# Attention units in runs of two: scores with queries, then values with projections, with single-buffered group data

## Chip, cores, metric

One core of one Trainium2 chip. The metric is the device time of one execution in microseconds (us), as the median of several executions. A difference counts as a change of speed only beyond 2%, but much of what follows is smaller than that and is read from the traces.

## The reference, cut

```
xn = layernorm(x)                                   # x: 2048 x 640
q  = xn @ wq                                        # 32 heads of 192
p  = softmax(q @ k.T * 192**-0.5)                   # the last 512 keys of the cache
s  = (p @ v) heads side by side @ wo                # 2048 x 6144 @ 6144 x 640
g  = silu((sigmoid(xn @ w_gate) * (xn @ w_up)) @ w_down)
out = x + s * g
```

## The kernel before

A preamble computes the gate `g`. The rest works in 32 *units*: 8 groups of 4 heads, times 4 blocks of 512 rows. For each unit the tensor engine (PE) does four kinds of work, each into one of four tiles `bank[0..3]` of PSUM, the memory that takes its results:

- `scores`: 8 groups of 6 matmuls on 64 rows of the array (two 64-row tiles work side by side: six matmuls in 0.65 us here, about 0.11 each; 34 full-row ones of the same width take 7.51 us in `a_warm` below, about 0.22 each); ScalarE (ACT) takes the exponential out of the bank.
- `queries` of a later unit: 6 halves of 10 matmuls, also on 64 rows; VectorE (DVE) copies the bank to `qT` (the cast).
- `values`: 4 heads of 16 matmuls on all 128 rows; DVE divides by the softmax sum.
- `project`: 4 tiles of 12 matmuls on 128 rows, which need the group's output weights `wo`; DVE adds to `acc`.

```python
for u in range(NU):
    ...
    if nxt:
        for i, what in enumerate(((0, 0), (1, 0), (0, 1), (1, 1), (2, 0), None, (2, 1), None)):
            scores(u, *sc[i], i % 2)                                    # banks 0, 1
            if what is not None:
                queries(u + 1, what[0], 2 + what[0] % 2, what[1])       # banks 2, 3, 2
    if b == 1 and g + 1 < NG:
        load_group(g + 1, nc.gpsimd)      # query weights, keys, values: two buffers
        load_wo(g + 1)                    # two buffers, POOL's queue
    if b == 2 and g + 1 < NG:
        turn_keys(g + 1)
    if nxt:
        order = (3, 2, 0, 1, 3, 2, 0, 1) if u else ...
        for q in range(4):
            values(u, q, order[2 * q])                                  # banks 3, 0, 3, 0
            if q == 3:
                turn_out(u)
            if u > 0:
                project(u - 1, q, order[2 * q + 1], nc.sync)            # banks 2, 1, 2, 1
# ... the last unit follows in an order of its own (the tail)
```

The softmax here doesn't subtract the row's maximum and nothing guards it: scores larger than these inputs give would overflow.

## Time and profile before

| before | |
|---|---|
| median of 3 runs | 931.14 us (930.13 to 931.9) |
| profiled span | 928.4 us |
| PE busy | 921.9 us (99%), clock 1.00 |
| DVE, ACT, POOL busy | 50%, 33%, 14% |
| one unit, start to start | 23.72 us |

The page's first part (busy time, share of the span, instructions) and its clock line:

```profile
PE 921.9 (99%) x8034; PEld 546.1 (59%) x8034; DVE 467.7 (50%) x739; ACT 304.9 (33%) x333; POOL 126.4 (14%) x154
...
PEclk9999999999999999999999999999999999999999
```

PE bounds the kernel. But 99% does not say that nothing is lost: the Trainium skill, "Perfetto Trace Analysis", opening note, calls matmul busy time a bad metric for the distance to the roofline, because matmuls are pipelined. The trace agrees: the windows view counts PE as busy in all 711.64 us from 187.83 to 899.47, drains included, and the drains described next cost time. So I read from start to start. The timeline of the kernel before, PE only, around both borders of a unit; columns are start, duration, what, and how many instructions:

```profile
280.99 1.79 PE L445 MATMUL bank<-wo_sb,oT 128*128 128x512 bf16 x12
282.71 0.82 PE L390 MATMUL bank<-qT,kT 64*128 64x512 bf16 x6
283.37 1.24 PE L408 MATMUL bank<-xnT,wq_sb 64*128 64x512 bf16 x10
284.45 0.81 PE L390 MATMUL bank<-qT,kT 64*128 64x512 bf16 x6
285.10 1.24 PE L408 MATMUL bank<-xnT,wq_sb 64*128 64x512 bf16 x10
...
291.35 1.46 PE L390 MATMUL bank<-qT,kT 64*128 64x512 bf16 x12
292.65 1.24 PE L408 MATMUL bank<-xnT,wq_sb 64*128 64x512 bf16 x10
293.73 0.81 PE L390 MATMUL bank<-qT,kT 64*128 64x512 bf16 x6
294.47 1.51 PE L425 MATMUL bank<-vbuf,E 128*128 128x193 bf16 x16
295.81 1.79 PE L445 MATMUL bank<-wo_sb,oT 128*128 128x512 bf16 x12
297.44 1.50 PE L425 MATMUL bank<-vbuf,E 128*128 128x193 bf16 x16
```

L390 is scores, L408 queries, L425 values, L445 projections. A projection tile takes 1.63 us inside its run (295.81 to 297.44) and 1.72 before scores (280.99 to 282.71). A score group takes 0.65 us inside its run (284.45 to 285.10; two take 1.30, 291.35 to 292.65) and 0.74 before values (293.73 to 294.47). So each turn between 64-row and 128-row work costs about 0.09 us. The Trainium skill, "TensorEngine Tiling (Array Packing)", Key Properties, says that changing the tiling mode drains the engine; this is what that looks like here. And one line of DVE in the same timeline, the cast of the unit's last query:

```profile
293.93 1.23 DVE L415 CAST qT<-bank 128x1024 bf16<-128x1024 f32 x1 [2.21 <-PE bank L408]
```

It holds its bank until 295.16, after the first value head has started (294.47). That does no harm, because here the cast empties bank 2 and the value head writes bank 3.

### The profile page before, as it was taken

Reading aid. Unit: us, or ns where it says so; the run is one execution under the profiler, and the core shown is the slowest. Engines: PE = TensorE matmul, PEld = TensorE weight load, DVE = VectorE, ACT = ScalarE, POOL = GpSimd, SP = SyncE. Lnnn points to the kernel's source line nnn. Section 1 sums busy time; section 2 is a strip of 40 time slices with the busy share of each in tenths; the row PEclk is TensorE's granted clock in tenths of the full one; section 3 lists DMA queues with packets and bytes.
Section 4 is the critical chain, followed back from the end, with each engine's and each line's share of the span. In section 5 each row is a group of like instructions: output and inputs, shape, how many; then the busy total and the mean of one; then the engine's idle time right before and its main releaser. Section 6 shows DMA issues by size and latency. Waiting matters only on the chain.

```text
span 928.4 us, 18112 instructions
## 1 busy us (share of the span) xinstructions
PE 921.9 (99%) x8034; PEld 546.1 (59%) x8034; DVE 467.7 (50%) x739; ACT 304.9 (33%) x333; POOL 126.4 (14%) x154
## 2 busy tenths in 40 slices
PE   9999999999999999999999999999999999999997
PEld 6445455565666556666556666556666666666665
DVE  5452522455545545445545445544555555445657
ACT  4222222433333333333333333333333333333341
POOL 1000100400010001000200020002000205555000
PEclk9999999999999999999999999999999999999999
DMA  9310420616224423443353433263326234422223
GB/s 319 79 29 1 130 43 1 196 36 146 52 53 78 129 60 60 78 96 92 61 77 62 119 69 78 57 124 69 78 49 131 69 68 77 93 63 64 53 64 102
DMA packets 157824, 76.69 MB, mean 83 GB/s; under 512 B 140801, under 2 KB 151665, under 8 KB 157745
## 3 DMA queue, kind: packets, MB, share of 16 engines
q1 hardware_dynamic: 149264, 45.90, 24.6%
q0 software_dynamic: 7248, 28.38, 10.7%
q8 instruction: 63, 1.03, 0.5%
q10 hardware_dynamic: 1232, 1.25, 0.4%
q14 instruction: 17, 0.13, 0.1%
HBM read 39.45 MB, written 2.62 MB: 45 GB/s over the span
## 4 chain that ended last, share of the span: by engine, by line
PE 98%; DVE 1%; DMA 1%; issue 0%; ACT 0%; DVEq 0%
PE bank L408 22%; PE bank L445 21%; PE bank L425 19%; PE bank L390 18%; PE bank L241 10%; PE bank L253 6%; PE bank L291 1%; PE bank L358 1%; DVE gate L454 1%; DMA wg_sb<-in_B_w_gate_dram 1%; DVE o_sb L449 1%; PE bank L221 0%; ACT xnT L227 0%; DVEq L530 0%; DVE warm L156 0%
## 5 line engine op out<-in xcount | busy, mean ns | idle before, releaser
L394 ACT ACTIVATE E<-bank 128x1024 bf16<-128x1024 f32 x256 | 257.8, 1023 | 477.4 <-PE bank L390 465.6
L408 PE MATMUL bank<-xnT,wq_sb 64*128 64x512 bf16 x1860 | 231.4, 376 | 0.0
L445 PE MATMUL bank<-wo_sb,oT 128*128 128x512 bf16 (+1 forms) x1536 | 228.6, 299 | 0.0
L390 PE MATMUL bank<-qT,kT 64*128 64x512 bf16 x1536 | 202.2, 377 | 0.0
L425 PE MATMUL bank<-vbuf,E 128*128 128x193 bf16 x2048 | 191.0, 247 | 0.0
L425 PEld LDWEIGHTS <-E 128*128 128x128 bf16 x2048 | 167.8, 98 | 24.2 <-issue 13.6
L415 DVE CAST qT<-bank 128x1024 bf16<-128x1024 f32 x93 | 113.9, 1225 | 132.8 <-PE bank L408 132.8
L445 PEld LDWEIGHTS <-oT 128*128 128x128 bf16 x1536 | 121.1, 98 | 76.8 <-issue 0.4
L408 PEld LDWEIGHTS <-wq_sb 64*128 64x128 bf16 x1860 | 97.3, 100 | 104.5
L390 PEld LDWEIGHTS <-kT 64*128 64x128 bf16 x1536 | 73.1, 94 | 90.0 <-issue 8.8
L431 DVE TENSOR_TENSOR o_st<-bank,rden 128x768 bf16<-128x768 f32 x128 | 122.6, 958 | 4.8 <-DVE rden L430 0.4
L460 DVE TENSOR_TENSOR acc<-bank,acc 128x640 f32<-128x640 f32 x96 | 79.2, 825 | 44.1 <-PE bank L445 44.1
L413 DVE COPY seen<-bank 128x2 f32<-128x2 f32 x93 | 14.8, 160 | 93.9 <-PE bank L408 93.8
L430 DVE RECIPROCAL rden<-bank 128x4 f32<-128x4 f32 x128 | 23.4, 182 | 71.0 <-PE bank L425 70.8
L241 PE MATMUL bank<-xnT,wg_sb 128*128 128x512 bf16 x220 | 54.7, 379 | 0.0
L241 PE MATMUL bank<-xnT,wu_sb 128*128 128x512 bf16 x220 | 54.7, 379 | 0.0
L253 PE MATMUL bank<-wd_sb,hT 128*128 128x512 bf16 (+1 forms) x384 | 52.8, 299 | 0.0
L247 DVE TENSOR_TENSOR hT<-bank,sig 128x512 bf16<-128x512 f32 x44 | 30.3, 689 | 42.2 <-ACT sig L244 42.2
L244 ACT ACTIVATE sig<-bank 128x512 bf16<-128x512 f32 x44 | 26.3, 597 | 68.4 <-PE bank L241 63.7
L106 POOL DMA_DIRECT2D vbuf<-in_A_v_cache_dram x28 | 20.9, 747 | 184.9 <-PE bank L425 184.9
L253 PEld LDWEIGHTS <-hT 128*128 128x128 bf16 x384 | 29.6, 98 | 23.2
L241 PEld LDWEIGHTS <-wu_sb 128*128 128x128 bf16 x220 | 21.5, 98 | 26.0
(51 smaller groups left out, 277.2 us busy)
## 6 DMA issues: line engine op xcount, KB each, us to landing
wo_sb<-in_A_wo_dram POOLq DMA_DIRECT2D x8, 960.0 KB, 7.3
wq_sb<-in_A_wq_dram POOLq DMA_DIRECT2D x7, 960.0 KB, 6.2
k_st<-in_A_k_cache_dram POOLq DMA_DIRECT2D x7, 768.0 KB, 7.9
vbuf<-in_A_v_cache_dram POOLq DMA_DIRECT2D x28, 192.0 KB, 3.0
row<-in_A_x_dram POOLq DMA_DIRECT2D x16, 160.0 KB, 2.6
oT<-o_st SPq DMA_TRANSPOSE x128, 2.6
x_sb<-in_A_x_dram SPq DMA_DIRECT2D x3, 640.0 KB, 11.0
wd_sb<-in_B_w_down_dram SPq DMA_DIRECT2D x1, 1920.0 KB, 14.5
```

The lines of the kernel that those rows point to most:

```text
L241: nc.tensor.matmul(bank[k][:, half, 0:r1 - r0], lhsT=w[:, c, f * P:(f + 1) * P], rhs=xnT[:, b, c, r0:r1], start=(c == 0), stop=(c == NCD - 1))
L244: nc.scalar.activation(sig[:, 0:r1 - r0], bank[k][:, 0, 0:r1 - r0], AF.Sigmoid)
L247: nc.vector.tensor_tensor(hT[b][:, f, r0:r1], bank[k][:, 1, 0:r1 - r0], sig[:, 0:r1 - r0], ALU.mult)
L253: nc.tensor.matmul(wide(k)[:, d0:d1], lhsT=hT[b][:, f, q * P:(q + 1) * P], rhs=wd_sb[:, f, d0:d1], start=(f == 0), stop=(f == NF - 1))
L390: nc.tensor.matmul(bank[k][:, i, :], lhsT=kT[r, pr, j, c * P:(c + 1) * P], rhs=q[r, pr * DJ + j, :], start=(j == 0), stop=(j == DJ - 1))
L394: nc.scalar.activation(E[u, pr][:, c, :, :], bank[k][:], AF.Exp, scale=scale_qk)
L408: nc.tensor.matmul(bank[k][:, half, :], lhsT=wq[r, c, col:col + DJ * (P - 1) + 1:DJ], rhs=xnT[r, b, c, :], start=(c == 0 and not second), ...
L415: nc.vector.tensor_copy(qT[u][:, 2 * m:2 * m + 2, :], bank[k][:])
L425: nc.tensor.matmul(o4[:, q, 0:DH + 1], lhsT=e[:, c, h % 2, q * P:(q + 1) * P], rhs=v[:, h, c, 0:DH + 1], start=(c == 0), stop=(c == KC - 1))
L431: nc.vector.tensor_tensor(o_st[u][:, :, h * DH:(h + 1) * DH], o4[:, :, 0:DH], rden[:].to_broadcast([P, TQ, DH]), ALU.mult)
L445: nc.tensor.matmul(wide(k)[:, d0:d1], lhsT=oT[u][:, cc, q * P:(q + 1) * P], rhs=wo[:, cc, d0:d1], start=(cc == 0), stop=(cc == GC - 1))
L460: nc.vector.tensor_tensor(acc[:, t, :], wide(k)[:, 0:D], acc[:, t, :], ALU.add)
```

## The change

Its intent: work in runs of two units, so that PE turns between the two kinds of work half as often. That needs more buffers for exponentials, queries and outputs, and the space comes from making all group data single-buffered. The query banks alternate between 2, 3, 2 and 3, 2, 3, so that the second unit of a run need not wait for the first one's last cast. The output weights move to SyncE's queue. The last two units form the tail.

```diff
-    vbuf = [pers.tile([P, 4, KC, VP], BF16, name=f"vbuf{i}") for i in range(2)]
+    vbuf = pers.tile([P, 4, KC, VP], BF16, name="vbuf")
 ...        (query weights, turned keys and staged keys likewise: one buffer)
-        nc.gpsimd.dma_start(d["wo"][:], wo_r[:, g * GC:(g + 1) * GC, :])
+        nc.sync.dma_start(d["wo"][:], wo_r[:, g * GC:(g + 1) * GC, :])
 ...        (the preamble computes the queries of units 0 and 1)
-    wo_pool = ctx.enter_context(tc.tile_pool(name="wo_pool", bufs=2))
+    wo_pool = ctx.enter_context(tc.tile_pool(name="wo_pool", bufs=1))
 ...        (E: 4 buffers, qT: 4, o_st: 2; rows of the residual: 2 instead of 4)
+    order = (3, 2, 0, 1)
+    for u0 in range(0, NU - 2, 2):
+        g, second = u0 // NB, u0 % NB != 0
+        more = g + 1 < NG
+        for u in (u0, u0 + 1):
             for i, what in enumerate(((0, 0), (1, 0), (0, 1), (1, 1), (2, 0), None, (2, 1), None)):
                 scores(u, *sc[i], i % 2)
                 if what is not None:
-                    queries(u + 1, what[0], 2 + what[0] % 2, what[1])
+                    queries(u + 2, what[0], 2 + (what[0] + u) % 2, what[1])
+        if more and not second:
+            load_wq(g + 1, nc.gpsimd)
+            load_keys(g + 1, nc.gpsimd)
+        if more and second:
+            turn_keys(g + 1)
+        for u in (u0, u0 + 1):
             for q in range(4):
+                if u0 > 0:
+                    values(u, q, order[2 * q % 4])
+                    project(u - 2, q, order[(2 * q + 1) % 4], nc.sync)
+                else:
+                    values(u, q, order[q])
+            turn_out(u)
+        if more and second:
+            load_values(g + 1, nc.gpsimd)
+        if g > 0 and not second:
+            load_wo(g)
+    u = NU - 2                                   # the tail: units 30 and 31
+    sc = [(v, *s) for v in (u, u + 1) for s in sc]
+    for i in range(6):
+        scores(*sc[i], order[i % 4])
+    for q in range(2):
+        project(u - 2, q, q, nc.sync)
 ...        (the rest of the scores, projections and values)
```

More of the change, by code (lines that the diff above doesn't have):

```diff
@@ L64 @@
     pers = ctx.enter_context(tc.tile_pool(name="pers", bufs=1, **rs))
-    load2 = ctx.enter_context(tc.tile_pool(name="load2", bufs=2, **rs))
     load1 = ctx.enter_context(tc.tile_pool(name="load1", bufs=1, **rs))
-    qpool = ctx.enter_context(tc.tile_pool(name="qpool", bufs=2, **rs))
+    qpool = ctx.enter_context(tc.tile_pool(name="qpool", bufs=4, **rs))
     bank = [psum.tile([P, 2, 512], F32, name=f"bank{i}") for i in range(4)]
@@ L91, with load_wq, load_keys, load_values @@
     grp = {}
-    def load_group(g, eng):
+    kv = slice(Sk - W, Sk)
+    def load_wq(g, eng):
         d = grp.setdefault(g, {})
-        d["wq"] = load2.tile([P, NCD, GW], BF16, name="wq_sb")
+        d["wq"] = load1.tile([P, NCD, GW], BF16, name="wq_sb")
         eng.dma_start(d["wq"][:], wq_r[:, :, g * GW:(g + 1) * GW])
-        kst = load1.tile([P, 4, KC, DH], BF16, name="k_st")
-        kv = slice(Sk - W, Sk)
-        eng.dma_start(
-            kst[:].rearrange("p h j d -> p h (j d)"),
-            A_k_cache[0, 4 * g:4 * g + 4, kv, :].rearrange("h (p j) d -> p h (j d)", j=KC),
-        )
-        d["v"] = vbuf[g % 2]
+    def load_keys(g, eng):
+        kp = load1.tile([P, 2, KC, DJ, P], BF16, name="k_perm")
+        for pr in range(2):
+            kst = load1.tile([P, 2, KC, DH], BF16, name="k_st")
+            h0 = 4 * g + 2 * pr
+            eng.dma_start(
+                kst[:].rearrange("p h j d -> p h (j d)"),
+                A_k_cache[0, h0:h0 + 2, kv, :].rearrange("h (p j) d -> p h (j d)", j=KC),
+            )
+            for i in range(2):
+                nc.gpsimd.tensor_copy(
+                    kp[:, pr, :, :, i * H2:(i + 1) * H2],
+                    kst[:, i, :, :].rearrange("p c (i j) -> p c j i", j=DJ),
+                )
+        grp[g]["kp"] = kp
+    def load_values(g, eng):
         for h in range(4):
             eng.dma_start(
-                d["v"][:, h, :, 0:DH],
+                vbuf[:, h, :, 0:DH],
                 A_v_cache[0, 4 * g + h, kv, :].rearrange("(p j) d -> p j d", j=KC),
             )
-        kp = load1.tile([P, 2, KC, DJ, P], BF16, name="k_perm")
-        for h in range(4):
-            nc.gpsimd.tensor_copy(
-                kp[:, h // 2, :, :, (h % 2) * H2:(h % 2) * H2 + H2],
-                kst[:, h, :, :].rearrange("p c (i j) -> p c j i", j=DJ),
-            )
-        d["kp"] = kp
     def load_wo(g):
@@ L120, in load_wo @@
         d["wo"] = wo_pool.tile([P, GC, D], BF16, name="wo_sb")
-        nc.gpsimd.dma_start(d["wo"][:], wo_r[:, g * GC:(g + 1) * GC, :])
+        nc.sync.dma_start(d["wo"][:], wo_r[:, g * GC:(g + 1) * GC, :])
     def turn_keys(g):
         d = grp[g]
-        d["kT"] = load2.tile([P, 2, DJ, W], BF16, name="kT")
+        d["kT"] = load1.tile([P, 2, DJ, W], BF16, name="kT")
         for pr in range(2):
@@ L175 @@
         make_identity(nc, ident[:])
-        for i in range(2):
-            nc.gpsimd.memset(vbuf[i][:, :, :, DH:DH + 2], 1.0)
+        nc.gpsimd.memset(vbuf[:, :, :, DH:DH + 2], 1.0)
         def dummy(n):
@@ L343 @@
             if b == 2:
-                load_group(0, nc.sync)
+                load_wq(0, nc.sync)
+                load_keys(0, nc.sync)
+                load_values(0, nc.sync)
             if b == 3:
@@ L359, in query_psum @@
                                  rhs=xnT[:, b, c, :], start=(c == 0), stop=(c == NCD - 1))
-        qT[0] = qpool.tile([P, 2 * DJ, TB], BF16, name="qT")
-        for m in range(DJ):
-            for half in range(2):
-                query_psum(0, 2 * m + half, k, half)
-            nc.vector.tensor_copy(qT[0][:, 2 * m:2 * m + 2, :], bank[k][:])
-            k = (k + 1) % 4
-    wo_pool = ctx.enter_context(tc.tile_pool(name="wo_pool", bufs=2))
+        for u in range(2):
+            qT[u] = qpool.tile([P, 2 * DJ, TB], BF16, name="qT")
+            for m in range(DJ):
+                for half in range(2):
+                    query_psum(u, 2 * m + half, k, half)
+                nc.vector.tensor_copy(qT[u][:, 2 * m:2 * m + 2, :], bank[k][:])
+                k = (k + 1) % 4
+    wo_pool = ctx.enter_context(tc.tile_pool(name="wo_pool", bufs=1))
     acc_pool = ctx.enter_context(tc.tile_pool(name="acc_pool", bufs=1))
-    e_pool = ctx.enter_context(tc.tile_pool(name="e_pool", bufs=2))
-    o_pool = ctx.enter_context(tc.tile_pool(name="o_pool", bufs=1))
+    e_pool = ctx.enter_context(tc.tile_pool(name="e_pool", bufs=4))
+    o_pool = ctx.enter_context(tc.tile_pool(name="o_pool", bufs=2))
     oT_pool = ctx.enter_context(tc.tile_pool(name="oT_pool", bufs=2))
     small = ctx.enter_context(tc.tile_pool(name="small", bufs=4))
-    fin = ctx.enter_context(tc.tile_pool(name="fin", bufs=4))
+    fin = ctx.enter_context(tc.tile_pool(name="fin", bufs=2))
     acc = acc_pool.tile([P, NT, D], F32, name="acc")
@@ L419, in values @@
     def values(u, h, k):
-        g = u // NB
-        v, e = grp[g]["v"], E[u, h // 2]
+        e = E[u, h // 2]
         o4 = wide(k).rearrange("p (q n) -> p q n", q=TQ)
@@ L425, in values @@
                 nc.tensor.matmul(o4[:, q, 0:DH + 1], lhsT=e[:, c, h % 2, q * P:(q + 1) * P],
-                                 rhs=v[:, h, c, 0:DH + 1], start=(c == 0), stop=(c == KC - 1))
+                                 rhs=vbuf[:, h, c, 0:DH + 1], start=(c == 0), stop=(c == KC - 1))
         if h == 0:
@@ L465, in project @@
             nc.gpsimd.tensor_tensor(acc[:, t, :], acc[:, t, :], x_sb[:], ALU.add)
-    for u in range(NU):
-        g, b = u // NB, u % NB
-        nxt = u + 1 < NU
-        sc = [(pr, c) for pr in range(2) for c in range(KC)]
-        if nxt:
+    sc = [(pr, c) for pr in range(2) for c in range(KC)]
+    order = (3, 2, 0, 1)
[3 more added lines that the diff above has]
+        for u in (u0, u0 + 1):
             for i, what in enumerate(((0, 0), (1, 0), (0, 1), (1, 1), (2, 0), None, (2, 1), None)):
@@ L474 @@
                 if what is not None:
-                    queries(u + 1, what[0], 2 + what[0] % 2, what[1])
-        if b == 1 and g + 1 < NG:
-            load_group(g + 1, nc.gpsimd)
-            load_wo(g + 1)
-        if b == 2 and g + 1 < NG:
+                    queries(u + 2, what[0], 2 + (what[0] + u) % 2, what[1])
[3 more added lines that the diff above has]
+        if more and second:
             turn_keys(g + 1)
-        if nxt:
-            order = (3, 2, 0, 1, 3, 2, 0, 1) if u else (3, None, 2, None, 0, None, 1, None)
+        for u in (u0, u0 + 1):
@@ L483 @@
             for q in range(4):
-                values(u, q, order[2 * q])
-                if q == 3:
-                    turn_out(u)
-                if u > 0:
-                    project(u - 1, q, order[2 * q + 1], nc.sync)
-    u = NU - 1
-    for i, k in enumerate((3, 2, 0, 1, 3, 2)):
-        scores(u, *sc[i], k)
-    project(u - 1, 0, 0, nc.sync)
-    scores(u, *sc[6], 1)
-    scores(u, *sc[7], 3)
-    for h, k in enumerate((2, 0, 1, 3)):
-        values(u, h, k)
-    turn_out(u)
-    for q, k in ((1, 2), (2, 0), (3, 1)):
-        project(u - 1, q, k, nc.sync)
@@ L502 @@
-    for q, k in ((0, 3), (1, 2), (2, 0)):
-        project(u, q, k, nc.scalar)
-    project(u, 3, 1, None)
+                if u0 > 0:
[10 more added lines that the diff above has]
+    sc = [(v, *s) for v in (u, u + 1) for s in sc]
@@ new lines @@
+    for i in range(6):
+        scores(*sc[i], order[i % 4])
+    for q in range(2):
+        project(u - 2, q, q, nc.sync)
+    for i in range(6, 12):
+        scores(*sc[i], order[(i - 6) % 4])
+    for q in range(2, 4):
+        project(u - 2, q, q - 2, nc.sync)
+    for i in range(12, 16):
+        scores(*sc[i], order[i % 4])
+    for q in range(4):
+        project(u - 1, q, order[q], nc.sync)
+    for v in (u, u + 1):
+        for h in range(4):
+            values(v, h, order[h])
+        turn_out(v)
@@ L508 @@
+    for q in range(4):
+        project(u, q, order[q], nc.sync)
+    for q in range(4):
+        project(u + 1, q, order[q], nc.scalar if q < 3 else None)
 _INS = ['A_x', 'A_k_cache', 'A_v_cache', 'A_wq', 'A_wo', 'B_x', 'B_w_gate', 'B_w_up', 'B_w_down']
```

## The prediction

> **What bounds the kernel.** The tensor engine. The page gives PE 921.9 of 928.4 us (99%), clock full in every slice, and the chain of waits is 98% PE. Busy time of matmuls is modelled, so I read start-to-start times from the timeline. One attention unit takes 23.72 us (starts of the first score group at 258.99 and 282.71). Inside it a score group takes 0.648 us, a query half 1.08, a value head 1.34, a projection tile 1.63: 8x0.648 + 6x1.08 + 4x2.97 = 23.54. So only 0.18 us per unit is lost, all at the two turns between 64-row work (scores, queries) and 128-row work (values, projections): score to value start is 0.74 instead of 0.65 (293.73 to 294.47), projection to score start 1.72 instead of 1.63 (280.99 to 282.71). The Trainium skill, "TensorEngine Tiling (Array Packing)", Key Properties, says that a change of tiling mode drains the engine; the trace agrees, at about 0.09 us a turn. No PE wait in the waits table is above 1.2 us in total; DVE (50%), ACT (33%), POOL (14%) and DMA have slack.
>
> **What the change does.** Matmul work is the same (unit 1's queries move to the preamble). Runs of two units cut the turns from 65 to 35, tail included: 30 x 0.09 = 2.7 us saved. All on the critical path.
>
> **What it adds.** For the second (odd) unit of a run the query banks are 3, 2, 3, so the last query of the run goes to bank 3; one score group later the first value head of the run is written to bank 3 too. Before, the last query was in bank 2 and the first value in bank 3. The cast that empties the bank starts 1.28 us after that query half starts and takes 1.23 us (292.65, 293.93, 295.16); the value head would start 1.82 us after it. So PE waits about 0.7 to 0.75 us for DVE at each of 15 score-to-value turns: about 11 us (estimate from those durations). The instruction order shows that the first value matmul waits for DVE. Once, at the start, the preamble's last cast is in bank 2, which the first query needs: 0.8 us.
>
> **What should stay hidden.** In-run exps (1.02 us in a 1.72 us step), the unit border inside a run (exp of group 6 ends about 0.2 us before bank 0 is needed). Single buffers: query weights (6.2 us to landing) must land within a value run of 23.7 us (10.7 us in the first, margin about 3.5); keys turned (11 us for 8 transposes) within 23.7; values and output weights within a score run of 23.5. The tightest is the values of the last group: they sit on POOL behind eight residual tiles at about 4.2 us each, so they should land some 3 us before use. The tail has the same matmuls.
>
> **Time.** 931.1 - 2.7 + 11.2 + 0.8 = 940.4 us, range 934 to 945. Chances: faster by 2% 0.01, within 2% 0.94, slower by 2% 0.05.
>
> **What will show it.** Waits table: PE value line waiting for DVE query cast, about 15 times, 0.7 us each, 11 us in total; PE busy lower by that. Timeline: score run 23.5 us, then last score start to first value start about 1.5 us instead of 0.74; the turn back 1.72. Score, query, value and projection steps unchanged.
>
> **What would make it wrong.** If the wait is largely covered (the cast starts earlier, or PE can begin values otherwise), the time is about 929. If a single-buffered load lands late (query weights, or the last values behind POOL), each exposes some us per group, and the time passes 945.

## The result, and the profile after

| | before | after |
|---|---|---|
| median of 4 runs each | 931.52 us (930.13 to 932.95) | 948.47 us (946.92 to 948.65) |
| ratio | | 1.0178 (95%: 1.0159 to 1.0197) |
| profiled span | 928.4 us | 946.9 us |
| PE busy | 921.9 us | 916.8 us (97%), clock 0.995 |

A ratio is the mean time of one kernel's fast runs over that of the other's fast runs of the same rounds, so it is not quite the ratio of the medians.

The change is slower by 1.8%: above my range (934 to 945), though still inside 2%. The waits table of the kernel after; columns are who waited for what, us in total, times, longest. In the table of before no row of a PE matmul reaches more than 1.2 us, and none names a cast or the output weights.

```profile
PE bank L431 <- DVE qT L422: 10.1, 15, 0.7
PEld L451 <- DMA wo_sb<-in_A_wo_dram: 7.9, 1, 7.9
PE bank L451 <- DMA wo_sb<-in_A_wo_dram: 7.4, 1, 7.4
PE bank L415 <- DVE qT L372: 0.6, 1, 0.6
```

The first and last rows were predicted: 15 waits of values for the cast, and one at the start of the loop. The 7.4 us for `wo_sb` was not. The predicted wait in the timeline, the border that answers to 292.65 to 295.81 of before (L397 scores, L415 queries, L431 values, L451 projections):

```profile
283.04 1.24 PE L415 MATMUL bank<-xnT,wq_sb 64*128 64x512 bf16 x10
284.12 0.81 PE L397 MATMUL bank<-qT,kT 64*128 64x512 bf16 x6
284.32 1.22 DVE L422 CAST qT<-bank 128x1024 bf16<-128x1024 f32 x1 [2.21 <-PE bank L415]
...
285.60 1.49 PE L431 MATMUL bank<-vbuf,E 128*128 128x193 bf16 x16 [0.67 <-DVE qT L422]
```

The step from the last score group to the first value head is now 1.48 us instead of 0.74. The cast ends at 285.54 and the value head starts 0.06 us later. Now the wait that was not predicted, in the timeline of the tail (the kernel after):

```profile
884.87 4.06 PE L397 MATMUL bank<-qT,kT 64*128 64x512 bf16 x36
896.31 0.71 PE L451 MATMUL bank<-wo_sb,oT 128*128 128x512 bf16 x2 [7.38 <-DMA wo_sb<-in_A_wo_dram]
897.24 4.34 PE L451 MATMUL bank<-wo_sb,oT 128*128 128x128 bf16 x21 [0.22 <-issue]
901.52 4.06 PE L397 MATMUL bank<-qT,kT 64*128 64x512 bf16 x36
```

Six score groups, then 7.4 us of nothing, then two projection tiles that take 5.21 us (896.31 to 901.52) instead of 2 x 1.63. The chain of waits says where the weights were (start, length, what):

```profile
884.94 0.77 PE bank L397 x6
885.71 0.47 SPq L443
...
888.89 1.29 SPq L443
890.17 0.04 issue
890.22 6.04 DMA wo_sb<-in_A_wo_dram
896.26 0.05 issue
896.31 0.71 PE bank L451 x2
```

SPq L443 is SyncE's queue issuing the four output transposes of unit 29, about 1.3 us each. The load stands behind them, starts at 890.22 and takes 6.04 us. It could not start before the projections of the previous group had ended (about 884.8), because there is one buffer. The clock in the slow stretch, from the windows view of the kernel after (busy us by engine, then clock, DMA share, GB/s):

```profile
896.31:901.52 5.21, 4.99 (x25) 2.54 (x26) 1.62 (x2) 0.00 (x0) 1.39 (x1) 0.64 0.01 3
```

The granted clock was 0.64 there on average, and 1.00 in the 560 us of loop before it. Finer windows show that the average hides two levels:

```profile
888.93:893.28 4.35, 0.00 (x1) 0.00 (x0) 0.00 (x0) 2.46 (x3) 3.28 (x4) 1.00 0.89 203
893.28:896.31 3.03, 0.00 (x0) 0.00 (x1) 0.00 (x0) 0.00 (x0) 2.36 (x3) 0.50 0.78 268
896.31:900.10 3.79, 3.57 (x14) 1.86 (x16) 0.30 (x1) 0.00 (x0) 1.39 (x1) 0.50 0.02 4
900.10:901.52 1.42, 1.42 (x14) 0.68 (x11) 1.32 (x2) 0.00 (x0) 0.00 (x0) 1.00 0.00 0
```

The clock fell to half 4.35 us after PE had stopped, and was full again 3.79 us after PE had resumed. The Trainium skill, "TensorE: Matmul & The Clock Gate", Part 1, says that the clock is halved after about 3.4 us of idling and comes back after as long a busy stretch; here it was 4.35 and 3.79 us, so this trace agrees roughly.

**The sum.** The profiled spans differ by 18.5 us. In us: 11.1 for 15 longer steps into values (15 x 0.74), 0.6 for the first query, 7.4 for the weights, 1.8 for the slow projections (5.21 minus the 3.37 that the same two take in `a_wo2` below), 0.8 by which the loop started late, and 3.3 gained by 30 fewer turns (at 0.11 each, measured in `b_turns` below). 11.1 + 0.6 + 7.4 + 1.8 + 0.8 - 3.3 = 18.4. The 0.8 is the first score group at 177.8 instead of 170.6 us, less the 6.5 us of unit 1's queries. It changes from run to run with the first gate weights: the same start was at 176.7 to 181.1 us in the profiles of the variants below.

### The profile page after: what moved, and what is told of

It is laid out like the page before. It is cut to its first block, busy times and chain, and to the rows that moved or that the text cites. A ratio compares the mean times of both kernels' runs of the same rounds, so it can differ in the third digit from the quotient of the medians.

```text
span 946.9 us, 17959 instructions
## 1 busy us (share of the span) xinstructions
PE 916.8 (97%) x7925; PEld 550.4 (58%) x8004; DVE 466.9 (49%) x736; ACT 302.6 (32%) x333; POOL 125.4 (13%) x152
## 4 chain that ended last, share of the span: by engine, by line
PE 94%; DVE 3%; DMA 1%; issue 1%; SPq 0%; DVEq 0%; ACT 0%
PE bank L451 21%; PE bank L415 21%; PE bank L431 18%; PE bank L397 16%; PE bank L245 10%; PE bank L257 5%; DVE qT L422 2%; PE bank L364 1%; PE bank L295 1%; DMA wg_sb<-in_B_w_gate_dram 1%; DVE gate L460 1%; DVE o_sb L455 1%; DMA wo_sb<-in_A_wo_dram 1%; SPq L443 0%; DVE qT L372 0%
## 5 line engine op out<-in xcount | busy, mean ns | idle before, releaser
L451 PE MATMUL bank<-wo_sb,oT 128*128 128x128 bf16 (+1 forms) x1475 | 225.0, 298 | 10.7 <-DMA wo_sb<-in_A_wo_dram 7.4
L415 PE MATMUL bank<-xnT,wq_sb 64*128 64x512 bf16 x1800 | 224.1, 376 | 0.6 <-DVE qT L372 0.6
L431 PE MATMUL bank<-vbuf,E 128*128 128x193 bf16 x2048 | 189.3, 247 | 10.1 <-DVE qT L422 10.1
L397 PE MATMUL bank<-qT,kT 64*128 64x512 bf16 x1536 | 198.7, 377 | 0.0
L431 PEld LDWEIGHTS <-E 128*128 128x128 bf16 x2048 | 169.7, 98 | 27.8 <-issue 16.1
L422 DVE CAST qT<-bank 128x1024 bf16<-128x1024 f32 x90 | 110.2, 1225 | 128.5 <-PE bank L415 128.5
L451 PEld LDWEIGHTS <-oT 128*128 128x128 bf16 x1536 | 121.6, 98 | 86.9 <-DMA wo_sb<-in_A_wo_dram 7.9
L415 PEld LDWEIGHTS <-wq_sb 64*128 64x128 bf16 x1800 | 94.3, 100 | 101.8 <-issue 0.8
L397 PEld LDWEIGHTS <-kT 64*128 64x128 bf16 x1536 | 74.9, 94 | 88.8 <-issue 4.8
L257 PE MATMUL bank<-wd_sb,hT 128*128 128x128 bf16 (+1 forms) x376 | 52.4, 298 | 0.4
## 6 DMA issues: line engine op xcount, KB each, us to landing
wd_sb<-in_B_w_down_dram SPq DMA_DIRECT2D x1, 1920.0 KB, 13.6
```

Source lines behind the costliest of these rows:

```text
L257: nc.tensor.matmul(wide(k)[:, d0:d1], lhsT=hT[b][:, f, q * P:(q + 1) * P], rhs=wd_sb[:, f, d0:d1], start=(f == 0), stop=(f == NF - 1))
L397: nc.tensor.matmul(bank[k][:, i, :], lhsT=kT[r, pr, j, c * P:(c + 1) * P], rhs=q[r, pr * DJ + j, :], start=(j == 0), stop=(j == DJ - 1))
L415: nc.tensor.matmul(bank[k][:, half, :], lhsT=wq[r, c, col:col + DJ * (P - 1) + 1:DJ], rhs=xnT[r, b, c, :], start=(c == 0 and not second), ...
L422: nc.vector.tensor_copy(qT[u][:, 2 * m:2 * m + 2, :], bank[k][:])
L431: nc.tensor.matmul(o4[:, q, 0:DH + 1], lhsT=e[:, c, h % 2, q * P:(q + 1) * P], rhs=vbuf[:, h, c, 0:DH + 1], start=(c == 0), stop=(c == KC ...
L451: nc.tensor.matmul(wide(k)[:, d0:d1], lhsT=oT[u][:, cc, q * P:(q + 1) * P], rhs=wo[:, cc, d0:d1], start=(cc == 0), stop=(cc == GC - 1))
```

## Experiments

Two causes were suspected, each with rivals. Every variant gave the correct result.

### a_bank: another bank order for the value runs

```diff
+    vorder = (2, 3, 0, 1)
-                    values(u, q, order[2 * q % 4])
-                    project(u - 2, q, order[(2 * q + 1) % 4], nc.sync)
+                    values(u, q, vorder[2 * q % 4])
+                    project(u - 2, q, vorder[(2 * q + 1) % 4], nc.sync)
-                    values(u, q, order[q])
+                    values(u, q, vorder[q])
```

Expected: 

> The changed kernel with only the bank order of the value runs turned to 2, 3, 0, 1, so that no value head starts in the bank that the last query cast is emptying. Bank theory (the 15 waits of 0.67 us on the cast are all lost time): the waits vanish and the time falls by about 10 us, from 948.5 to 938.4; the tail's wait for output weights (7.4 us) stays. Rival (the turn itself drains for that long and the cast is only the last semaphore to come): the step from last score group to first value head stays at 1.49 us and the time stays at 948.

Measured: 937.4 us (936.77 to 939.77). The waits for the cast are gone, and the timeline of `a_bank` shows the old step of 0.75:

```profile
284.19 0.81 PE L397 MATMUL bank<-qT,kT 64*128 64x512 bf16 x6
284.94 1.51 PE L431 MATMUL bank<-vbuf,E 128*128 128x193 bf16 x16
```

So the bank was the cause. It was worth 11.1 us between medians (948.47 to 937.4). The two were taken in different rounds, and by their ratios to the kernel before (1.0178 and 1.0066) it is about 10.4; so the times alone do not tell 15 x 0.74 from the 10.1 that the waits table totals. The steps in the two traces do: 1.48 and 0.75. The tail's wait for weights stayed, at 7.8 us.

### a_wo2: a second buffer for the output weights

```diff
-    qpool = ctx.enter_context(tc.tile_pool(name="qpool", bufs=4, **rs))
+    qpool = ctx.enter_context(tc.tile_pool(name="qpool", bufs=3, **rs))
-    wo_pool = ctx.enter_context(tc.tile_pool(name="wo_pool", bufs=1))
+    wo_pool = ctx.enter_context(tc.tile_pool(name="wo_pool", bufs=2))
         if more and second:
             turn_keys(g + 1)
+            load_wo(g + 1)
-        if g > 0 and not second:
-            load_wo(g)
```

With four query buffers the program does not build (not enough on-chip memory). Three are enough: the fourth unit's first cast comes after the first unit's scores are done.

Expected: 

> The changed kernel with only the output weights given a second buffer (paid for by three instead of four query buffers) and loaded one run of two units earlier. Weights theory: the 7.4 us wait in the tail and the half-speed projections after it (about 1.9 us) go: 948.5 to about 939.2, granted clock 1.00 in the tail; the 15 waits on the cast stay at 10 us. Rival (the tail is slow for its new order of work, not for the weights): the projections of the tail still wait or run slow, gain under 3 us.

Measured: 938.63 us (938.29 to 938.72), 9.8 us less than the change by the medians and about 9.0 by the ratios (1.0178 and 1.0081). The tail in the timeline of `a_wo2`:

```profile
883.80 4.06 PE L397 MATMUL bank<-qT,kT 64*128 64x512 bf16 x36
887.79 3.43 PE L451 MATMUL bank<-wo_sb,oT 128*128 128x512 bf16 x23
891.16 4.06 PE L397 MATMUL bank<-qT,kT 64*128 64x512 bf16 x36
```

No wait, and two projections in 3.37 us. So it was not the tail's new order of work that cost the time, but the late weights.

### a_both: both repairs (run twice)

The edit is the two above together.

Expected: 

> Both repairs. If the two causes add and the fewer turns are worth 2.7 us, the time is about 929 us, that is 2 to 3 us (0.2 to 0.3%) below the kernel before; if the turns are worth nothing it is 931 to 932; if some single-buffered load of keys, query weights or values also costs time it stays above 934.

Measured: 927.78 us (927.47 to 928.58) against 930.36 for the kernel before on the same chip, ratio 0.9967 (0.9954 to 0.998). The causes add, and what is left is a gain of 2.6 us.

Expected of the second run: 

> The two repairs once more, on the same chip as the run beside it, so that 0.6 us can be told: 927.8 us as before, one wait of 0.6 us on the preamble's cast.

Measured: 927.48 us (927.4 to 927.75) against 930.13, ratio 0.9967 (0.9955 to 0.998).

### a_noalt: query banks as before

```diff
-                    queries(u + 2, what[0], 2 + (what[0] + u) % 2, what[1])
+                    queries(u + 2, what[0], 2 + what[0] % 2, what[1])
```

Expected: 

> The changed kernel with the query banks as in the kernel before (2, 3, 2 in every unit). The last query of a run is then in bank 2 and the first value head in bank 3, so the 10 us of waits before the values go; but inside a run the second unit's first query needs bank 2 while the cast of the first unit's last query empties it: the cast ends about 2.5 us after that query half starts and the next one would start 2.37 us after it, so some 0.15 to 0.25 us at each of 15 places, about 3 us. Bank theory: about 941 us. Rival (alternation is not the cause): 948.

Measured: 939.98 us (939.1 to 940.96). The waits of values are gone, and a smaller loss is there instead, inside the run (the waits table has no row for it; the steps show it). In the timeline of `a_noalt`, the border between two units of a run (two score groups, then the next unit's first query):

```profile
270.51 1.46 PE L397 MATMUL bank<-qT,kT 64*128 64x512 bf16 x12
271.99 1.26 PE L415 MATMUL bank<-xnT,wq_sb 64*128 64x512 bf16 x10
```

1.48 us where two groups take 1.30: 0.18 x 15 = 2.7 us, which is the difference from `a_bank` (2.6). So the alternation removed a wait of 0.18 us inside the run and made one of 0.74 at its end, because the order of the value banks was left as it was.

### a_wofirst: the load ahead of the transposes

```diff
+            if g > 0 and not second and u > u0:
+                load_wo(g)
             turn_out(u)
-        if g > 0 and not second:
-            load_wo(g)
```

Expected: 

> The changed kernel with the load of the output weights put ahead of the second unit's four output transposes on SyncE's queue, still one buffer. Theory: of the 7.4 us wait in the tail 5.2 us is the queue (four transposes issued before the load) and the rest is the transfer against the 3.9 us of scores; so the wait falls to about 2.2 us[...], and the time goes from 948.5 to about 941.4. Rival (the transfer itself is slow on this queue): wait stays above 5 us, time above 945.

Measured: 942.74 us (940.54 to 947.33). The wait for the weights fell to 2.3 us, as expected, so 5.1 us of it was the queue. But the clock fell all the same. The windows view of `a_wofirst` over the two projections after the wait:

```profile
894.50:899.52 5.02, 5.02 (x24) 2.49 (x24) 1.59 (x2) 0.14 (x1) 0.35 (x1) 0.66 1.31 135
```

5.02 us at clock 0.66: the expected 941.4 us had left no time for a lowered clock, and that part failed. Finer windows put the fall at 894.7 us, 0.2 us after PE had resumed, and the return 3.4 us later. In this profiled run (the 947.33) the loop also started late, at 181.1 us, for the first gate weights. The four runs differ: the fastest, 940.54 us, has a mean clock of 1.000 over the execution, the other three 0.997 or 0.998. So the clock seems to have stayed up in that one; it left no trace.

### a_wopool: the weights on POOL's queue again

```diff
-        nc.sync.dma_start(d["wo"][:], wo_r[:, g * GC:(g + 1) * GC, :])
+        nc.gpsimd.dma_start(d["wo"][:], wo_r[:, g * GC:(g + 1) * GC, :])
```

Expected: 

> The changed kernel with the output weights loaded by POOL again, at the same place, one buffer. Theory: moving the load to SyncE is not the fault; on POOL the last load would stand behind the residual tiles, which end at 898.2 us in the trace of the changed kernel, so it would land near 905.5 us and the tail's wait grows from 7.4 to about 16.6 us: about 957 to 958 us. Rival (SyncE's queue is the fault of the change): faster than 945.

Measured: 955.92 us (954.34 to 958.96). The tail's wait grew to 14.5 us (16.6 expected), with the load issued at 896.6 behind the residual tiles. It would be wrong to blame SyncE's queue: with one buffer, POOL's is worse.

### a_warm: useless matmuls during the wait

```diff
+    for _ in range(34):
+        nc.tensor.matmul(bank[0][:, 0, :], lhsT=xnT[:, 0, 0, 0:P], rhs=xnT[:, 0, 0, :],
+                         start=True, stop=True)
     for q in range(2):
         project(u - 2, q, q, nc.sync)
```

Expected: 

> The changed kernel with 34 useless full-row matmuls (0.216 us each, 7.3 us in all) ahead of the first projection of the tail, so that the engine works while the weights travel. Theory: the wait's 7.4 us is still lost (as useless work), but the clock stays up and the two projections after it take 1.63 us each instead of 2.55: about 1.9 us less, 946.6, granted clock of the execution 1.00 instead of 0.995. Rival (the slow projections are slow for another reason, such as their weights' own arrival): still 5.1 us for the two and 948.5 or more.

Measured: 946.67 us (945.94 to 950.28). The times alone do not settle it: the ratio to the kernel before, 1.0184, is no better than the change's 1.0178: one run of the five took 950.28 us. The trace does. In the timeline and the windows view of `a_warm`:

```profile
888.14 7.51 PE L510 MATMUL bank<-xnT 128*128 128x512 bf16 x34
...
896.10 3.42 PE L451 MATMUL bank<-wo_sb,oT 128*128 128x512 bf16 x24 [0.44 <-DMA wo_sb<-in_A_wo_dram]
899.45 4.06 PE L397 MATMUL bank<-qT,kT 64*128 64x512 bf16 x36
```

```profile
896.10:899.45 3.35, 3.35 (x25) 1.79 (x25) 1.35 (x2) 0.00 (x0) 1.82 (x2) 1.00 0.05 20
```

The weights come as late, but with PE kept busy the same two projections take 3.35 us at clock 1.00 instead of 5.21 at 0.64. The slow projections were the clock, not the data.

### b_turns: more turns in the kernel before

```diff
     def queries(u, m, k, second):
 ...
+        if m == 2:
+            query_psum(u, 2 * m + second, k, second)      # five full-row matmuls
+            if second:
+                nc.vector.tensor_copy(qT[u][:, 2 * m:2 * m + 2, :], bank[k][:])
+            return
```

Expected: 

> The kernel before with the third pair of query columns of each unit computed by full-row matmuls (five per half, the same 1.08 us) at the same two places between score groups: the same matmul time, but four more turns between 64-row and 128-row work in each of 31 units. Drain theory at 0.09 us a turn: 31 x 4 x 0.09 = 11.2 us more, about 942 us. Rival (the 0.18 us per unit at the two run borders is not the change of tiling but waits that happen to sit there): within 2 us of 931.

Measured: 943.76 us (943.61 to 944.24) against 930.12, ratio 1.0146 (1.0132 to 1.016). 13.6 us for 124 turns is 0.11 us a turn, a little more than the 0.09 read from the trace. In the timeline of `b_turns`:

```profile
267.61 0.81 PE L390 MATMUL bank<-qT,kT 64*128 64x512 bf16 x6
268.35 1.26 PE L358 MATMUL bank<-xnT,wq_sb 128*128 128x512 bf16 x5
269.54 1.47 PE L390 MATMUL bank<-qT,kT 64*128 64x512 bf16 x12
```

0.74 us into the full-row query instead of 0.65, and 1.19 out of it instead of 1.08. The turn itself has a price, wherever it stands.

### a_best: both repairs, and the preamble's queries one bank on

```diff
+        k = (k + 1) % 4
         for u in range(2):
             qT[u] = qpool.tile([P, 2 * DJ, TB], BF16, name="qT")
```

(on top of the edits of `a_bank` and `a_wo2`.)

Expected: 

> Both repairs and the queries of the preamble moved on by one bank, so that the preamble's last cast is not in the bank that the first query of the loop needs. The one wait of 0.6 us on that cast should go: about 927.2 us against 927.8 for the two repairs alone, 0.3 to 0.4% below the kernel before. If the 0.6 us is taken up elsewhere: 927.8.

Measured: 926.93 us (926.54 to 927.3) against 930.13, ratio 0.996 (0.9947 to 0.9974); beside it on the same chip `a_both` took 927.48. The wait of 0.6 us is gone. This is the fastest version: 0.4% below the kernel before, less than what counts as faster, but clear of noise. Its 3.2 us fit the 30 saved turns: 3.3 at the 0.11 us of `b_turns`, 2.7 at the 0.09 of single borders.

## Why the prediction was wrong

- **What bounds it, and the gain** were right: PE bounds the kernel and the turns were a loss to win back. Predicted 2.7 us for 30 turns; `a_best` shows 3.2 and `b_turns` gives 0.11 us a turn.
- **The bank conflict** was right in place, number and size: predicted 0.7 to 0.75 us at each of 15 places, about 11 us; measured 0.74, and 10.4 to 11.1 us when `a_bank` removed it.
- **The first query** was right: 0.8 predicted, 0.6 measured.
- **The step that failed** is in "What should stay hidden": "values and output weights within a score run of 23.5". That holds for the weights of groups 1 to 6, which have a whole score run between their load and their first projection. It does not hold for the last group, whose first projection is in the tail, after six score groups: 3.9 us. I wrote that "the tail has the same matmuls", which is true, and did not ask there what each of them waits for. The load needs 5.4 us of queue (884.8 to 890.22; `a_wofirst` took 5.1 off the wait) and 6.0 of transfer. Missing terms: 7.4 us of wait and 1.8 us of lowered clock. With these 9.2 us the predicted 940.4 would have been 949.6, against 948.47 measured.
- **What I named as the danger** under "what would make it wrong" was a late single-buffered load, but I looked for it in the query weights and the last values. Neither shows a PE wait in the trace of the kernel after. The last values were issued at 850.2 us, behind the eight residual tiles, and were there in time.

What is not settled: how short an idle stretch lowers the clock (2.3 us did it in the profiled run of `a_wofirst`, and seemingly not in its fastest run), and what sets how long it stays low. The traces show 3.4, 6.8 and 13.7 us at half clock around waits of 2.3, 7.4 and 14.5 us (`a_wofirst`, the kernel after, `a_wopool`).

## What to carry to other kernels

When a buffer is made single, compute for *every* user of it the time from the last use of the old contents to the first use of the new, and look at the last round apart: here it was shortest in the tail, which has an order of its own. When a bank rotation is changed in one stage, check both borders of the stage: the bank that is written last here is still being emptied when the next stage starts. A stall of the tensor engine can be paid for twice: here the work after 7.4 us of it, and in one traced run after 2.3 us, began at half clock.

## What the Trainium skill lacked or had wrong

- "TensorEngine Tiling (Array Packing)", Key Properties, names the drain at a change of tiling mode but gives no cost. Here it is 0.11 us a turn between 64-row and 128-row work (13.6 us for 124 turns), 0.09 read from single borders.
- "TensorE: Matmul & The Clock Gate", Part 1, puts the fall of the clock after about 3.4 us without work. In one profiled run here 2.3 us of idling was followed by 5.02 us at a mean clock of 0.66 (`a_wofirst`: half clock from 0.2 us after work had resumed, for 3.4 us); after 7.4 us of idling it was 0.64 over 5.21 us.
- I found on no page how soon a matmul starts once the engine that empties its bank is done: here 0.06 us after the end of the cast (285.54 to 285.60, one border).
